# An attention and mixture-of-experts kernel: one rounding on another engine, one group of maxima and the weight loads at other places

## The chip, the core and the metric

The kernel runs on one core of a Trainium2 chip. The metric is the device time of one execution in microseconds; the runs shown are three executions of the kernel before, and one more that was profiled.

## What is computed

The input is 8 batches of 8 heads, 576 positions, 64 channels. Attention is causal with a decay, and its output, read as 4608 tokens of 512 channels, goes through a soft mixture of 8 experts with 4 slots each:

```
scores = (q @ k.T) / sqrt(64) + cum[i] - cum[j]      # cum = cumsum(log f); j > i is masked
attn   = softmax(scores); y = attn @ v               # per head
x      = y.transpose(0, 2, 1, 3).reshape(4608, 512)
logits = x @ phi                                     # 32 slots
slots  = softmax(logits over tokens).T @ x
out    = softmax(logits over slots) @ (relu(slots @ w1) @ w2)
```

## The kernel before

Heads are worked on in pairs: 32 pairs `g`, four to a batch, head `i` = 2g or 2g+1. All work is written out by hand in the order in which each engine takes it; the order of the code is the order of every engine's queue, and semaphores alone join the engines.

For a head there are two products. The first (`s1`, line 230) gives scores with queries on partitions, of which VectorE takes a maximum for each query (`tops`, lines 244 and 246, a group of instructions into `MT`, each with a short read-out of its own). `first(i, n)` is both for one of four groups of blocks. The maxima of a pair are turned into a row on TensorE (`mturn`, line 256), copied on ScalarE to `mr`, and carried by a DMA into a row of `YA` (`mrows`, lines 265 and 268). The second product (`s2`, lines 283 and 284) gives scores with keys on partitions; it uses that row to subtract the maximum. ScalarE makes exponentials of them (`expo`, line 290), GpSimd sets what lies above the diagonal to zero (`causal`, lines 298 and 301), and TensorE multiplies with the values (`s3`, line 315) 50 units for a pair, each in two passes. `both(i, n)` is `s2` and `expo` of a quarter.

The products are made of a rounded part and a rest. `round_k` and `round_q` (lines 183 and 188, ScalarE) round `RAW` into `WA` and `YA`; `dup_k` and `dup_q` (lines 199 and 203) copy these by DMA into `WB` and `YB`; `low_k` and `low_q` (lines 209 and 214, GpSimd) subtract to get the rests. `load_cum` (line 194) brings the cumulated logarithms.

The opening handles heads 0 and 1, the maxima of heads 2 to 4, and the values of pair 0. Behind it a loop over g = 1 to 31 does `s2` and `s3` of pair g beside the maxima of later heads. All loads and copies are issued by SyncE (SP) from one queue, in the order written. `wload(n)` (line 128) brings one of 27 weight tiles, 128 partitions of 4096 bytes, used only by the experts after the loop. In an iteration, SyncE's queue holds `RAW` of pair g+3 and `V` of pair g+1, a weight tile, the row of maxima, the logarithms of pair g+3, and the two copies of pair g+2.

Of the kernel before, what the change touches and what calls it, by code (L numbers as in the profile page):

```python
# [28 lines left out]
NRES = 27  # L29
# [19 lines left out]
def pt_col(c, i):  # L49
    at = {}  # L50
    for bank, cc, i0, w in SEGS:
        o = at.get(bank, 0)
        at[bank] = o + w
        if cc == c and i0 <= i < i0 + w:
            return SEG_O[bank] + o + i - i0
    raise ValueError


def queries(t, u):

    if t == 4:
        return 8
    return 2 * u + t if t < 2 else 4 + 2 * (1 - u) + t - 2


def units(h, u, ts):

    return [(h, t, u, c) for t in ts for c in range(queries(t, u) // 2 + 1)]


SIDES = [[x for n in zip(units(h, 0, range(4)), units(h, 1, range(4))) for x in n] for h in range(2)]
LAST = [units(h, h, (4,)) for h in range(2)]
# [3 lines left out]
def attn_softmoe(ctx: ExitStack, tc: tile.TileContext, qk, v, f, phi, w1, w2, cst, out):  # L76
    nc = tc.nc
# [21 lines left out]
    YA, WA, YB, WB = {}, {}, {}, {}  # L99
# [6 lines left out]
    RAW = [per.tile([P, 2, S], F32, name=f"RAW{i}") for i in range(3)]  # L106
# [19 lines left out]
    def wload(n):  # L126
        i, q = divmod(ORDER[n], 4)
        nc.sync.dma_start(quarter[n], (w1, w2)[i % 2][i // 2][:, QW * q : QW * q + QW])
# [25 lines left out]
    def pair(g):  # L154
        return 0 <= g < NG

    def head(i):
        return 0 <= i < NH
# [17 lines left out]
    def load_v(g):  # L176
        if pair(g):
            nc.sync.dma_start(V[:, g % 2], v[g])

    def round_k(g, *hs):  # L180
        if pair(g):
            for h in hs or range(2):
                nc.scalar.copy(WA[g % 3][0:64, S * h : S * h + S], RAW[g % 3][64:128, h])  # L183

    def round_q(g, *hs):
        if pair(g):
            for h in hs or range(2):
                nc.scalar.copy(YA[g % 3][0:64, h, 64:640], RAW[g % 3][0:64, h])  # L188
# [12 lines left out]
    def dup_q(g, h0=0, h1=2):  # L201
        if pair(g):
            nc.sync.dma_start(YB[g % 2][0:64, h0:h1].bitcast(F32), YA[g % 3][0:64, h0:h1, 64:640].bitcast(F32))
# [55 lines left out]
    def mrows(g, h0=0, h1=2):  # L259

        if not pair(g):
            return
        n = NBLK * (h1 - h0)
        mr = small.tile([2 * NBLK, P], F32R, name=f"mr{g}_{h0}", tag="mr", bufs=1)
        nc.scalar.copy(mr[0:n], st["pm", g, h0][0:n, 0:128])
        m = TOP[g % 3]
        dst = YA[g % 3][m : m + 1, h0:h1].rearrange("c h s -> c (h s)")
        nc.sync.dma_start(dst.bitcast(F32), mr[0:n].bitcast(F32))
# [18 lines left out]
    def expo(i, bank):  # L287
        if head(i):
            t, at = st["bank"]
            nc.scalar.activation(PT[i % 2][:, SEG_O[bank] : SEG_O[bank] + at], t[:, 0:at], AF.Exp, scale=0.125)  # L290
# [20 lines left out]
    def s3(g, todo):  # L311
        for h, t, u, c in todo:
            r = queries(t, u)
            at = pt_col(c, 64 * r)
            nc.tensor.matmul(  # L315
                pvv[h][64 * u : 64 * u + 64, t, :], PT[h][:, at : at + 64], V[:, g % 2, c, 65 * h : 65 * h + 65], start=(c == 0), stop=(c == r // 2)
            )
# [190 lines left out]
    def warm(n, a, w=192):  # L508

        for _ in range(n):  # L510
            nc.tensor.matmul(ring[0][:, 0:w], a[:, 0:128], a[:, 0:w], start=True, stop=True)
# [87 lines left out]
    def first(i, n, busy=0):  # L599
        s1(i, *GROUPS[n])  # L600
        warm(busy, cs)
        tops(i, *GROUPS[n])

    def both(i, n):
        s2(i, *((0,), (1,), (2,), (3, 4, 5))[n])
        expo(i, n)
# [15 lines left out]
    both(0, 1)  # L622
    first(2, 0)
    both(0, 2)
    nc.vector.tensor_copy(YA[1][0:64, 1, 64:640], RAW[1][0:64, 1])
    next(r1)
    first(2, 1)
    next(r1)
    s2(0, 3, 4, 5)
    round_k(1, 1)  # L630
    expo(0, 3)
    dup_q(1, 1, 2)
    dup_k(1, 1, 2)
# [18 lines left out]
    first(3, 2)  # L652
    first(3, 3)
    round_k(2, 0)
    both(1, 3)
    causal(1)
    low_k(3)
    low_q(3)
    round_q(2, 0)
    s3(0, SIDES[0])  # L660
    mturn(1, 1, 2)
    mrows(1, 1, 2)
    first(4, 0)
    round_k(2, 1)
    round_q(2, 1)
    dup_q(2)
    dup_k(2)
    s3(0, LAST[0])
    norm(0)
    first(4, 1)  # L670
    s3(0, LAST[1] + SIDES[1][:8])
# [53 lines left out]
    for g in range(1, NG):  # L725
        h0, h1 = 2 * g, 2 * g + 1
        u0, u1 = h0 + 3, h0 + 4
        b, w = divmod(g - 4, NPAIR)
        c = b - 1 if w == 0 else b if (b, w) == (B - 2, 3) else None
        if g < 4:  # L730
            load_v(g + 1)
            load_qk(g + 3)
        else:
            load_qk(g + 3)
            load_v(g + 1)
        if 2 <= g < NRES + 2:
            wload(g - 2)
        if w == 1:
            weigh(b)
        low_q(h0 + 2)  # L740
        low_q(h1 + 2)
        s2(h0, 0)
        expo(h0, 0)
        norm(h0 - 1)
        if w == 1:
            mgroup(b)
        if w == 2:
            combine(b, 0)
        s1(u0, 2)
        tops(u0, 2)  # L750
        s2(h0, 1)
        expo(h0, 1)
        s1(u0, 3)
        tops(u0, 3)
        if 1 < g < NG - 1:
            px(g - 1, 0)
        s2(h0, 2)
        expo(h0, 2)
        if g == NG - 1:
            px(g - 1, 0)  # L760
        if g > 1:
            px(g - 1, 3)
        else:
            round_k(3, 0)
            round_q(3, 0)
        s1(u0, 0, 1)
        tops(u0, 0, 1)
        if g > 1:
            px(g - 1, 1)
        s2(h0, 3)  # L770
        if g > 1:
            xcopy(g - 1, (0, 3))
            px(g - 1, 2)
            xcopy(g - 1, (1, 2))
        s2(h0, 4)
        s1(u0, 4, 5)
        s2(h0, 5)
        expo(h0, 3)
        tops(u0, 4, 5)
        causal(h0)  # L780
        low_k(h0 + 2)
        if w == 1:
            mtop(b)
        s2(h1, 0)
        expo(h1, 0)
        if g == 1:
            for t in (0, 3, 1, 2):
                px(0, t)
        px(g - 1, 4)
        if g == 1:  # L790
            xcopy(0, (0, 3))
            xcopy(0, (1, 2))
        xcopy(g - 1, (4,))
        s1(u1, 2)
        tops(u1, 2)
        s2(h1, 1)
        expo(h1, 1)
        s1(u1, 3)
        tops(u1, 3)
        s2(h1, 2)  # L800
        if g < NG - 2:
            expo(h1, 2)
        mturn(g + 1)
        mrows(g + 1)
        if g >= NG - 2:
            expo(h1, 2)
        s1(u1, 0, 1)
        tops(u1, 0, 1)
        s2(h1, 3, 4)
        s1(u1, 4, 5)  # L810
        s2(h1, 5)
        expo(h1, 3)
        tops(u1, 4, 5)
        causal(h1)
        low_k(h1 + 2)
        if g == 1:
            round_k(3, 1)
            round_q(3, 1)
        load_cum(g + 3)
        dup_q(g + 2)  # L820
        dup_k(g + 2)
        if g == 29:
            sides[2].close()
            p2 = fresh(ctx, "p2", 2)
            wstream(*p2, RAW[30 % 3])
        if g == 30:
            sides[1].close()
            xp = ctx.enter_context(tc.tile_pool(name="xp", bufs=1))
            X.append(xp.tile([P, NBLK, 256], F32, name="X3"))
            p0 = fresh(ctx, "p0", 1)  # L830
            p1 = fresh(late, "p1", 3)
            wstream(*p0, *p1, RAW[31 % 3])
        if g == 31:
            sides[0].close()
            with tc.using_default_side("right"):
                tp = ctx.enter_context(tc.tile_pool(name="tp", bufs=1))
            cT = tp.tile([P, sum(CUT)], F32R, name="cT")
            wstream(tp.tile([P, QW], F32, name="w36"))
        if w == 1:
            mcast(b)  # L840
        if c is not None:
            combine(c, 1)
        if w == 2 and b < B - 2:
            dispatch(b, *range(NBLK))
        if g == NG - 1:
            st["lg", B - 1] = scratch(False, f"lg{B - 1}")
            nc.vector.memset(st["lg", B - 1][:, 128:192], -1.0e30)
        round_k(g + 3)
        if w == 1:
            weigh2(b)  # L850
            total(b)
        round_q(g + 3)
        if c is not None:
            combine(c, 2)
        s3(g, VALUES[:30])
        norm(h0)
        if g == 31:
            logits(B - 1, 0, 1)
            wstream(XTS[:, 0:QW], PTS[:, 0:QW])
            split(0, 0)  # L860
            split(1, 0)
        s3(g, VALUES[30:])
        if w == 0:
            logits(b, *range(NPAIR))
        if w == 1:
            tokens(b, 0, 1)
        if g == 28:
            wstream(RAW[29 % 3])
# [272 lines left out]
```

## Time and profile before

| what | value |
|---|---|
| time, median of three runs | 389.6 us (389.45 to 389.81) |
| time of the profiled execution | 392.3 us |
| its span, first to last instruction | 390.6 us |
| TensorE busy | 370.5 us, 95% of the span |
| VectorE, ScalarE, GpSimd busy | 281.7, 271.3, 255.0 us |
| DMA | 93.72 MB, mean 240 GB/s |

In the profile, PE is TensorE's matmuls and PEld its weight loads, which overlap; DVE is VectorE, ACT ScalarE, POOL GpSimd, SP SyncE (SPq: its queue, which issues DMAs). A busy share is a mean over stages with different limits, so it is read by stretches of time. A releaser in brackets is the work that ended a wait, as far as the semaphores' events tell.

### The profile page before, as it was taken

What the parts mean: (1) busy time and instruction counts of PE and PEld (TensorE: products, weight loads), DVE (VectorE), ACT (ScalarE), POOL (GpSimd) and SP (SyncE); (2) the same over time, 40 slices, a digit from 0 to 9 for tenths busy, and PEclk for the clock granted to TensorE, in tenths of its full rate; (3) what the DMA queues carried; (4) which work ended last, traced back from release to release, by engine and by line L of the source; (5) the groups of instructions that cost most, each with busy time, mean ns of one, the idle gap of its engine ahead of it and who ended that gap; (6) DMA issues with size and microseconds to landing.
All of it is one profiled execution on the core that took longest, in us unless ns stands there. A gap on an engine that the chain in (4) does not pass through costs nothing.

```text
span 390.6 us, 15123 instructions
## 1 busy us (share of the span) xinstructions
PE 370.5 (95%) x5863; PEld 330.7 (85%) x5863; DVE 281.7 (72%) x1080; ACT 271.3 (69%) x669; POOL 255.0 (65%) x357
## 2 busy tenths in 40 slices
PE   7999999999999999999999999999999998999870
PEld 7789999999999999999999999999999885567640
DVE  7978887878887788788878887878787534341681
ACT  8869887878787778787878787878786553021560
POOL 4897887878787878787878787878787821000000
PEclk9999999999999999999999999999999998999995
DMA  6875978777777777777777777777775899995798
GB/s 205 205 195 148 283 223 278 189 233 207 224 211 215 213 212 214 213 214 211 213 214 214 211 214 212 214 214 212 212 227 154 269 350 377 407 417 206 264 393 314
DMA packets 34344, 93.72 MB, mean 240 GB/s; under 512 B 4266, under 2 KB 8288, under 8 KB 34272
## 3 DMA queue, kind: packets, MB, share of 16 engines
q1 hardware_dynamic: 34272, 92.75, 76.4%
q8 instruction: 46, 0.75, 0.8%
q14 instruction: 26, 0.21, 0.2%
HBM read 63.93 MB, written 9.73 MB: 189 GB/s over the span
## 4 chain that ended last, share of the span: by engine, by line
PE 86%; DMA 6%; POOL 2%; DVE 1%; ACT 1%; issue 1%; POOLq 0%; DVEq 0%; ACTq 0%
PE pv L315 24%; PE ring L283 14%; PE s L230 13%; PE ring L284 13%; PE pv L342 5%; PE pv L981 4%; PE more L941 4%; PE lg L389 3%; DMA out<-RAW 3%; PE ds L475 2%; DMA YA<-mr 2%; DMA WB<-WA 1%; POOL WB L209 1%; DMA PTS<-in_f 1%; POOL YB L214 1%
## 5 line engine op out<-in xcount | busy, mean ns | idle before, releaser
L290 ACT ACTIVATE PTS<-ring 128x320 f32<-128x320 f32 (+2 forms) x256 | 118.1, 502 | 49.3 <-PE ring L284 36.4
L283 PE MATMUL ring<-YA,WA 67*128 67x320 f32 (+9 forms) x384 | 121.5, 330 | 0.8 <-DMA YA<-mr 0.8
L246 DVE CUSTOM_DVE_ANT_0 s<-s,mask 128x320 f32<-128x320 f32 (+3 forms) x256 | 109.0, 442 | 5.6 <-PE s L230 1.1
L284 PE MATMUL ring<-YB,WB 128*128 128x320 f32 (+4 forms) x384 | 110.4, 296 | 0.0
L315 PE MATMUL pv<-V,PTS 128*64 128x65 f32 x3200 | 101.9, 223 | 0.2 <-POOL WB L209 0.2
L315 PEld LDWEIGHTS pv<-V,PTS 128*64 128x64 f32 x3200 | 96.9, 138 | 3.1 <-issue 1.5
L230 PE MATMUL s<-WA,YA 66*128 66x288 f32 (+9 forms) x384 | 98.2, 310 | 0.8 <-DMA RAW<-in_qk 0.4
L209 POOL TENSOR_TENSOR WB<-RAW,WB 64x576 fp32r<-64x576 f32 x64 | 90.4, 1412 | 11.1 <-DMA WB<-WA 5.8
L214 POOL TENSOR_TENSOR YB<-RAW,YA 64x576 fp32r<-64x576 f32 x64 | 89.7, 1421 | 2.6 <-POOL EX L397 0.2
L283 PEld LDWEIGHTS ring<-YA,WA 67*128 67x128 f32 (+3 forms) x384 | 69.7, 183 | 6.3 <-issue 2.1
L284 PEld LDWEIGHTS ring<-YB,WB 128*128 128x128 f32 (+1 forms) x384 | 70.0, 182 | 0.1
L230 PEld LDWEIGHTS s<-WA,YA 66*128 66x128 f32 (+1 forms) x384 | 62.9, 190 | 7.4 <-ACT PTS L290 1.5
L301 POOL TENSOR_SCALAR_AFFINE_SELECT PTS<-PTS 128x128 f32<-128x128 f32 (+1 forms) x128 | 31.5, 268 | 21.1 <-ACT PTS L290 18.6
L246 DVE DVE_READ_ACCUMULATOR2_ANT MT<- 128x1 fp32r x310 | 43.8, 141 | 0.0
L298 POOL TENSOR_SCALAR_AFFINE_SELECT PTS<-PTS 128x384 f32<-128x384 f32 x64 | 33.5, 523 | 14.2 <-ACT PTS L290 10.3
L342 PE MATMUL pv<-cs,X 128*128 128x128 f32 x155 | 42.0, 277 | 0.0
L183 ACT CAST WA<-RAW 64x576 fp32r<-64x576 f32 x64 | 40.1, 668 | 1.0 <-DMA RAW<-in_qk 0.2
L188 ACT CAST YA<-RAW 64x576 fp32r<-64x576 f32 x63 | 39.6, 671 | 0.4
L246 DVE CUSTOM_DVE_ANT_0 s<-s,mask,MT 128x288 f32<-128x288 f32 x62 | 32.6, 526 | 9.3 <-PE s L230 0.4
L330 DVE TENSOR_SCALAR rl<-pv 128x5 f32<-128x5 f32 x64 | 10.5, 164 | 34.0 <-PE pv L315 23.6
L335 DVE TENSOR_TENSOR X<-pv,rl 128x320 f32<-128x320 f32 (+1 forms) x65 | 31.5, 486 | 2.4 <-DMA YA<-mr 0.3
L244 DVE TENSOR_REDUCE MT<-s 128x1 fp32r<-128x288 f32 x62 | 27.8, 449 | 0.4 <-PE s L230 0.4
(221 smaller groups left out, 389.2 us busy)
## 6 DMA issues: line engine op xcount, KB each, us to landing
w<-in_w SPq DMA_DIRECT2D x45, 512.0 KB
RAW<-in_qk SPq DMA_DIRECT2D x31, 576.0 KB
V<-in_v SPq DMA_DIRECT2D x32, 325.0 KB
YB<-YA SPq DMA_DIRECT2D x30, 288.0 KB
WB<-WA SPq DMA_DIRECT2D x30, 288.0 KB
p<-in_w SPq DMA_DIRECT2D x6, 512.0 KB
out<-RAW SPq DMA_DIRECT2D x6, 512.0 KB
out<-p SPq DMA_DIRECT2D x5, 512.0 KB
```

What stands on the lines that cost most here:

```text
L183: nc.scalar.copy(WA[g % 3][0:64, S * h : S * h + S], RAW[g % 3][64:128, h])
L188: nc.scalar.copy(YA[g % 3][0:64, h, 64:640], RAW[g % 3][0:64, h])
L209: nc.gpsimd.tensor_tensor(t[0:64], RAW[g % 3][64:128, h], t[64:128].bitcast(F32), op=ALU.subtract)
L214: nc.gpsimd.tensor_tensor(YB[g % 2][64:128, h], RAW[g % 3][0:64, h], YA[g % 3][0:64, h, 64:640].bitcast(F32), op=ALU.subtract)
L230: nc.tensor.matmul(t[:, o : o + w], ya[0:m, h, 128 * blk : 128 * blk + 128], wa[0:m, j0 : j0 + w], start=True, stop=True)
L246: nc.vector.tensor_tensor_reduce(out=t[:, o : o + w], in0=t[:, o : o + w], in1=mask[:, m0 : m0 + w], scale=1.0, scalar=top.bitcast(F32) if ...
L283: nc.tensor.matmul(o, wa[0:m, j0 : j0 + n], ya[0:m, h, 64 + i0 : 64 + i0 + w], start=True, stop=False)
L284: nc.tensor.matmul(o, wb[:, j0 : j0 + n], yb[:, h, i0 : i0 + w], start=False, stop=True)
L290: nc.scalar.activation(PT[i % 2][:, SEG_O[bank] : SEG_O[bank] + at], t[:, 0:at], AF.Exp, scale=0.125)
L298: nc.gpsimd.affine_select(d3, d3, pattern=[[0, 3], [1, 128]], compare_op=ALU.is_ge, fill=0.0, base=0, channel_multiplier=-1)
L315: nc.tensor.matmul(pvv[h][64 * u : 64 * u + 64, t, :], PT[h][:, at : at + 64], V[:, g % 2, c, 65 * h : 65 * h + 65], start=(c == 0), stop= ...
L342: nc.tensor.transpose(pm[:, 0:128], x[:, t, 128 * (p % 2) : 128 * (p % 2) + 128], ident)
```

## The change

Three edits. In the opening, the rounding of the second head of pair 1 goes from VectorE (line 625) to ScalarE, behind the rounding of its keys. Also in the opening, the rounding of the queries of pair 2's first head stands ahead of `both(1, 3)` and no longer behind it, and pair 2's first maxima, `first(4, 0)`, stand ahead of the turn of head 3's maxima; `SIDES[0]` has 20 units, so the values of pair 0 are cut as before. In the loop, `wload` is issued behind `mrows`.

```diff
     both(0, 2)
-    nc.vector.tensor_copy(YA[1][0:64, 1, 64:640], RAW[1][0:64, 1])
     next(r1)
     first(2, 1)
     next(r1)
     s2(0, 3, 4, 5)
     round_k(1, 1)
+    round_q(1, 1)
     expo(0, 3)
     dup_q(1, 1, 2)
...
     round_k(2, 0)
+    round_q(2, 0)
     both(1, 3)
     causal(1)
     low_k(3)
     low_q(3)
-    round_q(2, 0)
-    s3(0, SIDES[0])
+    s3(0, SIDES[0][:20])
+    first(4, 0)
     mturn(1, 1, 2)
     mrows(1, 1, 2)
-    first(4, 0)
     round_k(2, 1)
     round_q(2, 1)
     dup_q(2)
     dup_k(2)
-    s3(0, LAST[0])
+    s3(0, SIDES[0][20:] + LAST[0])
...
             load_v(g + 1)
-        if 2 <= g < NRES + 2:
-            wload(g - 2)
         if w == 1:
...
         mturn(g + 1)
         mrows(g + 1)
+        if 2 <= g < NRES + 2:
+            wload(g - 2)
```

ScalarE's queue in the opening, with the changes marked; `WA_86` and `YA_85` are pair 1's rounded keys and queries, the 512 wide `ACTIVATE` is `expo(0, 3)`:

```order
 L594 CAST YA_89<-ring_151 2x128
 L183 CAST WA_86<-RAW_96 64x576
+L188 CAST YA_85<-RAW_96 64x576
 L290 ACTIVATE PTS<-ring_152 128x512
 L290 ACTIVATE PTS<-ring_153 128x448
```

One instruction came in ahead of `expo(0, 3)`; VectorE's queue lost line 625 ahead of head 2's maximum of block 4.

TensorE's queue at the values of pair 0, with the changes marked; `s_0` is head 4's first group of scores, `pv_150<-turner` the turn of head 3's maxima:

```order
 L284 MATMUL ring_153<-YB_91,WB_92 64x64
 L315 MATMUL pv_149<-V,PTS 64x65 x20
+L230 MATMUL s_0_395<-WA_94,YA_93 128x320
+L230 MATMUL s_0_395<-WA_94,YA_93 128x192
 L256 MATMUL pv_150<-turner,MT_110 5x128
-L230 MATMUL s_0_399<-WA_94,YA_93 128x320
-L230 MATMUL s_0_399<-WA_94,YA_93 128x192
 L315 MATMUL pv_149<-V,PTS 64x65 x5
```

Two matmuls went from behind the turn to ahead of it.

SyncE's queue in the loop, at the end of pair 2 and in pair 3, with the changes marked; `mr` is the row of maxima, `w` a weight tile:

```order
 L178 DMA V<-in_v 128x650
 L174 DMA RAW_97<-in_qk 128x1152
+L268 DMA YA_89<-mr_0_681 1x10x128
 L128 DMA w_113<-in_w 128x1024
-L268 DMA YA_89<-mr_0_682 1x10x128
```

The weight tile went from ahead of the row of maxima to behind it, and so directly ahead of the logarithms and the two copies; the same holds in the 26 pairs that follow.

## Rows read from the trace of the kernel before

**Rows 1.** Windows: stretch, length, then each engine's busy time, PEclk, DMA share, GB/s

```profile
16.00:18.00 2.00, 1.63 (x12) 1.30 (x11) 1.85 (x5) 1.41 (x4) 1.86 (x6) 1.00 0.94 336
18.00:20.00 2.00, 1.72 (x10) 1.23 (x10) 1.90 (x9) 1.38 (x5) 1.84 (x5) 1.00 1.01 204
...
32.00:310.00 278.00, 276.98 (x4706) 260.15 (x4707) 220.51 (x881) 220.84 (x548) 225.50 (x307) 1.00 0.74 216
```

**Rows 2.** Waits of PE, 30 to 310 us: sum, times, longest

```profile
PE ring L283 <- DMA YA<-mr: 0.5, 1, 0.5
```

**Rows 3.** Timeline of DVE in the opening: start, length, instruction

```profile
15.43 1.32 DVE L625 CAST YA<-RAW 64x576 fp32r<-64x576 f32 x1
16.67 0.44 DVE L244 TENSOR_REDUCE MT<-s 128x1 fp32r<-128x288 f32 x1
...
18.61 0.14 DVE L246 DVE_READ_ACCUMULATOR2_ANT MT<- 128x1 fp32r x1
...
19.52 0.14 DVE L246 DVE_READ_ACCUMULATOR2_ANT MT<- 128x1 fp32r x1
```

**Rows 4.** Groups by line and form, DVE: busy us, mean ns, idle before

```profile
L557 DVE CAST PTS<-PTS 64x576 fp32r<-64x576 f32 x1 | 0.5, 457 | 0.0
```

**Rows 5.** Timeline of PE and PEld in the opening; in brackets idle time and releaser

```profile
16.94 0.19 PEld L230 LDWEIGHTS s<-WA,YA 66*128 66x128 f32 x1 [0.67 <-POOL YA L578]
...
18.13 0.49 PE L511 MATMUL ring<-cs 128*128 128x192 f32 x2
...
18.89 0.22 PE L256 MATMUL pv<-turner,MT 128*5 128x128 f32 x1 [0.28 <-POOL WB L209]
...
19.71 0.30 PEld L230 LDWEIGHTS s<-WA,YA 66*128 66x128 f32 x2 [0.23 <-DVE MT L246]
...
22.20 0.50 PE L230 MATMUL s<-WA,YA 66*128 66x320 f32 x2
```

**Rows 6.** Timeline of ACT in the opening

```profile
16.09 0.67 ACT L183 CAST WA<-RAW 64x576 fp32r<-64x576 f32 x1
16.67 0.59 ACT L290 ACTIVATE PTS<-ring 128x512 f32<-128x512 f32 x1
17.82 0.94 ACT L290 ACTIVATE PTS<-ring 128x448 f32<-128x448 f32 x2 [0.57 <-ACT PTS L290]
...
21.48 0.67 ACT L188 CAST YA<-RAW 64x576 fp32r<-64x576 f32 x1
```

**Rows 7.** Timeline of SP's queue and of POOL in the opening

```profile
16.78 0.47 SPq L203 DMA_DIRECT2D YB<-YA  x1
...
17.93 0.45 SPq L194 DMA_DIRECT2D WA<-cumd  x1
...
21.88 0.49 POOL L301 TENSOR_SCALAR_AFFINE_SELECT PTS<-PTS 128x128 f32<-128x128 f32 x2
```

**Rows 8.** Chain that ended last: start, length, work (DMA: issue to landing)

```profile
5.82 4.61 DMA WB<-WA
...
97.03 3.07 PE pv L315 x100
...
126.45 3.80 DMA YA<-mr
```

**Rows 9.** Windows of two stretches in the loop, columns as in rows 1

```profile
127.00:129.00 2.00, 2.00 (x76) 2.00 (x74) 1.05 (x6) 1.96 (x4) 1.83 (x4) 1.00 0.07 15
95.00:96.00 1.00, 1.00 (x9) 0.94 (x9) 0.83 (x4) 0.96 (x5) 0.75 (x3) 1.00 0.99 379
```

**Rows 10.** The page's DMA issues: count and size of one

```profile
w<-in_w SPq DMA_DIRECT2D x45, 512.0 KB
```

**Rows 11.** Timeline of SP's queue and of POOL in a short pair

```profile
90.10 1.48 SPq L199 DMA_DIRECT2D WB<-WA  x1
...
95.74 1.42 POOL L209 TENSOR_TENSOR WB<-RAW,WB 64x576 fp32r<-64x576 f32 x1
...
97.82 0.49 POOL L301 TENSOR_SCALAR_AFFINE_SELECT PTS<-PTS 128x128 f32<-128x128 f32 x2
```

## Prediction

> **What bounds the kernel now.** I read the busy time of each engine by stretches first. From 32 to 310 us, the attention loop, TensorE is busy for 276.98 of 278.00 us [rows 1]: there is about 1 us in it that any edit to the loop can take away. In the opening it is not so full: 1.63 us of the two from 16 to 18, and 1.72 of the two from 18 to 20 [rows 1], 0.65 us idle. So the change can only pay in these few microseconds of the opening, or in single waits of the loop. The list of TensorE's waits over the loop names one of note, 0.5 us for the row of maxima that a DMA carries from `mr` into `YA` [rows 2]. What is gained early is kept: TensorE is the bound behind it, and whatever follows starts earlier by as much.
>
> **Which engine holds TensorE in the opening.** VectorE makes the row maxima there one behind the other. Between two of them it does the rounding of line 625, from 15.43 us, for 1.32 us, and only at 16.67 takes the next maximum (head 2, block 4) [rows 3]. The same kind of copy with the same shape, line 557, took 0.457 us earlier [rows 4]. TensorE's first wait there, the weight load at 16.94, is for a GpSimd memset [rows 5], which the change leaves where it is. Two others stand behind VectorE. The turn of head 2's maxima (line 256) begins at 18.89 after 0.28 us of idleness [rows 5]; the last of those maxima is read out at 18.61 to 18.75 [rows 3]. (The timeline blames a GpSimd operation; the program makes this instruction wait for VectorE and for a copy of `turner` on GpSimd that is long done, so I take VectorE.) Then the weight load for head 3's block 3 stands still for 0.23 us, until 19.71, for a buffer that VectorE reads until 19.66 [rows 3, 5].
>
> **The rounding's move.** ScalarE gets one more instruction, line 188, which takes it 0.67 us at 21.48, as line 183 does at 16.09 [rows 6]. It stands behind line 183, which runs 16.09 to 16.76, so it ends at about 17.45. What is queued behind: `expo(0, 3)`, at 16.67 before, then about 17.46 to 18.05; `expo(1, 0)` behind it, 17.82 before, then about 18.07 [rows 6]. Head 3's first matmul needs the rounded rows; it comes near 17.57, so it loses nothing or a tenth. VectorE loses 1.24 us of work (15.43 to 16.67). It then must wait for matmuls in between, the last piece of head 2's block 0 among them, which waits for a GpSimd memset and doesn't come earlier; I put the end of head 2's maxima at about 17.8 in place of 18.75, and that of head 3's first group at about 19.1 in place of 19.66. So the 0.28 goes whole, and the 0.23 nearly whole: 0.28 + 0.23 = 0.51 us. The bounds: nothing, if another releaser takes over; at most 0.66, if the turn follows the filler matmul of 18.13 after 0.26 us [rows 5], at 18.39 (0.50 earlier), and the weight load gains 0.16 more.
>
> The SyncE queue waits for the rounding too: the copy of `YA` into `YB` is issued at 16.78, when VectorE is through, and the cumulated logarithms of pair 2 behind it at 17.93 [rows 7]. With ScalarE they go out about 0.68 us later, if nothing else holds the queue.
>
> **`round_q(2, 0)` and `first(4, 0)`.** Before, the rounding of pair 2's queries follows `expo(1, 3)`, at 21.48 to 22.15 [rows 6], and pair 2's first maxima begin at 22.20 [rows 5]: that start is set by ScalarE. Put ahead of `expo(1, 3)`, the rounding follows `round_k(2, 0)` and is done near 21.1; `expo(1, 3)` goes 0.67 us later than it else would, ends near 21.7 and is needed by GpSimd only at 21.88 [rows 7]. `first(4, 0)` can then follow the 40 passes of values without a stop, so the 0.5 us isn't lost again; I count no further gain for it. It swaps places with the turn of head 3's maxima, which go out a little later and are used only in the next pair; nothing.
>
> A rule of the Trainium skill bears on the rounding. The row says 1.32 us, with a GpSimd subtraction under way. The Trainium skill (SBUF — State Buffer, SBUF: two separate sides) says that VectorE and GpSimd share a port pair as an exclusive lock, and that ScalarE never waits on anyone there. By it VectorE would get back more than the bare copy, and ScalarE's price stays 0.67; the trace agrees, 1.32 against 0.457 us for one shape. By the bare copy alone, VectorE would be only 0.46 us earlier and the gain about 0.4 us.
>
> **The weights behind the row of maxima.** It removes nothing; in 27 pairs, 2 to 28, one issue on SyncE (about 0.44 us) and one transfer of 512 KB change places with the row's. SyncE's queue waits for ScalarE's `mr` anyway, so the row is issued no earlier. Does the row land earlier? In the one case where TensorE waited, it took 3.80 us from issue to landing [rows 8], but the DMA engines were busy for only 7% of the time from 127 to 129 us [rows 9]: the weights, issued at the pair's start, were through. So I give the move no gain there: 0, at most the 0.5.
>
> Its cost is what now stands behind the weights: the cumulated logarithms, and the copies `YB<-YA` and `WB<-WA` of the next pair. At the 379 GB/s of a full stretch [rows 9], the 512 KB [rows 10] take 1.38 us, part of which falls in the hole that the DMAs leave beside the row. So the copies land between 0.44 (the issue alone) and 1.8 us later (issue and transfer in full); I take 0.9. In a short pair `WB<-WA` is issued at 90.10, and GpSimd's subtraction `low_k` begins at 95.74, 5.64 later [rows 11]; the longest such copy on the chain took 4.61 us [rows 8], which leaves 1.03. Behind `low_k` stands the causal fill of the odd head, 97.82 to 98.31 [rows 11]. The value matmuls from 97.03 take 3.07 us for 100 passes [rows 8] and reach the first that needs it after 54, at 98.69: 0.38 us of room more. So 1.4 us of lateness cost nothing: 0 for my 0.9, and 0.4 us in each short pair for 1.8. I take seven such pairs, one a batch: 2.8 us at the worst. The next `RAW` stands behind the copies as well; there ScalarE would wait, and I put that under the same bound.
>
> The Trainium skill (DMA: Bandwidth & Descriptors, Queues, rings and completion order) says that a DMA engine consumes the descriptors of one ring in order. That speaks against this part of the change: bytes which nobody needs for long go ahead of copies that are. It is what the third rival is made of.
>
> **The sum.** 0.51 of the opening, nothing for the rest: the profiled execution would go from 392.3 us (its span is 390.6) to 391.8. The median of the runs shown is 389.6, 2.7 below the profiled one; less 0.5 it gives **389.1 us**.
>
> **The rivals.**
> - The wait for the row of maxima goes too, because its DMA no longer shares the engines with the weights: 0.5 + 0.5, 388.6 us. For it: it is the loop's only long wait. Against: the DMA engines were idle then. 20%.
> - The opening's gain is taken back. The queue's 0.68 us make pair 2's logarithms land later than `first(4, 0)` can use them; issued at 18.6, and landing as slowly as that 3.80, they would come at 22.4, past the 22.20 of before. Then only GpSimd's chain and this DMA set the opening: 389.5 to 389.7. Against: the DMAs there are backlogged (the share is 1.01 from 18 to 20 [rows 1]), so a later issue need not mean a later landing. 18%.
> - Slower: the copies behind the weights come more than 1.4 us late in the short pairs, GpSimd's fill holds the value matmuls, seven times 0.4 less 0.5: 391.9; 0.2 each, 390.5. The sign turns at 0.07 us a pair, and 0.18 make it slower by over 0.2%. For it: the transfers are dense in the loop (share 0.74 [rows 1]). Against: the hole beside the row takes part of the transfer. 12%.
> - My forecast, 50%, with 388.8 to 389.4 as its own range.
>
> **The numbers.** 0.2% of 389.6 is 0.78 us, about what a measurement of this kernel tells from no change. Faster than 388.8: the first rival's 20% and the low edge of my forecast, 7%, together 27%. Slower than 390.4: the third rival, 12%. The rest, 61%, is the same. The range must leave out no more than a tenth on either side: 388.4 below (the first rival and its 0.66 bound), 390.2 above (the third at its mild end).
>
> **What would show it.** In the changed profile VectorE should take head 2's first maximum of block 4 near 15.6, and line 256 should start without a wait near 18.4. Pair 2's first maxima should start near 21.7 in place of 22.20. The loop's busy share should stand as it was, and GpSimd's `low_k` should begin as soon behind its fill as before. I am wrong if line 256 still waits (then GpSimd was the releaser), if `first(4, 0)` waits for a DMA, or if waits on GpSimd turn up ahead of the value matmuls in every fourth pair.

## The result, and the profile after

The changed kernel takes **394.5 us** (median of 4, 393.41 to 395.73) where the kernel before, on the same chip, takes 389.58 (median of 4): 1.0126 of it, interval 1.0096 to 1.0157. It is slower by 4.9 us, and the prediction of 389.1 is wrong, past its range; what happened is the mechanism of the slower rival, which it had priced at 0.9 to 2.3 us over the kernel before. The profiled execution after has a span of 392.6 us. Against the 390.6 of before that looks like 2.0 only: before's profiled execution was 2.7 above its median, and from pair 31's start to the end it took 78.3 us against 77.0 after, with a granted clock of 0.93 from 310 to 330 us (a mean: from 328 to 330 us it was 0.50, the lower of its two levels, 1.2 GHz; after: 1.00).

The opening first: VectorE's timeline in the changed kernel (start, length, instruction).

```profile
15.55 0.46 DVE L244 TENSOR_REDUCE MT<-s 128x1 fp32r<-128x288 f32 x1
```

And TensorE's there (in brackets idle time and what ended it):

```profile
17.48 0.51 PE L230 MATMUL s<-WA,YA 66*128 66x320 f32 x2 [0.37 <-ACT YA L188]
...
18.34 0.36 PE L256 MATMUL pv<-turner,MT 128*5 128x128 f32 x1
...
21.45 0.50 PE L230 MATMUL s<-WA,YA 66*128 66x320 f32 x2
```

VectorE takes the maximum of block 4 at 15.55, not 16.67 [rows 3]; line 256 starts without a wait at 18.34 (18.89 [rows 5]) and pair 2's maxima at 21.45 (22.20 [rows 5]). One wait is new: head 3's matmul at 17.48 waits 0.37 us for ScalarE's rounding. Another is gone, that of 16.94 [rows 5], which I had expected to stay. Most of this is no work of the change, as "The opening again" below shows. Windows of the changed kernel, columns as in [rows 1]:

```profile
16.00:18.00 2.00, 1.63 (x11) 1.21 (x10) 1.46 (x7) 1.97 (x5) 1.85 (x5) 1.00 0.95 347
18.00:20.00 2.00, 2.00 (x17) 1.88 (x16) 1.37 (x6) 1.74 (x5) 1.92 (x4) 1.00 0.89 207
32.00:310.00 278.00, 275.22 (x4648) 258.18 (x4645) 218.95 (x874) 217.56 (x539) 221.26 (x301) 1.00 0.75 212
```

The opening's hole from 18 to 20 is closed, and the loop has lost: TensorE is busy for 275.22 us where it was busy for 276.98 [rows 1]. TensorE's waits in the changed loop, 30 to 310 us (sum, times, longest):

```profile
PE pv L315 <- POOL PTS L301: 1.5, 5, 0.5
PE ring L283 <- DMA YA<-mr: 0.8, 1, 0.8
```

And GpSimd's, of which the first profile of the kernel before has none of this kind (a second, below, has 0.5 us in two):

```profile
POOL WB L209 <- DMA WB<-WA: 8.9, 12, 1.8
```

TensorE's value matmuls now wait for GpSimd's fill, and GpSimd's `low_k` for the copy `WB<-WA`. (Three more waits of `low_k`, 3.1 us, the profile puts down to ScalarE's `mr`; by the completion marks these too end 0.14 us behind the last share of the copy.) The wait for the row of maxima is still there, at 0.8 us. The chain that ended last shows how the two hang together, in pair 8 (start, length, work):

```profile
90.10 6.29 DMA WB<-WA
...
96.52 1.42 POOL WB L209
...
98.00 0.52 POOL PTS L298
98.52 0.45 POOL PTS L301 x2
...
99.02 1.50 PE pv L315 x42
```

The copy goes out at 90.10, as it did before [rows 11], but lands 6.29 us later; `low_k` starts at 96.52, not 95.74 [rows 11], the fill behind it ends at 98.97, and the last 42 value matmuls stand until then. The same piece stands in the chain at 42.81, 129.34, 216.69, 246.78 and 286.33. TensorE's timeline at this place, in the kernel before and in the changed one:

```profile
96.96 3.14 PE L315 MATMUL pv<-V,PTS 128*64 128x65 f32 x100
```
```profile
96.58 1.96 PE L315 MATMUL pv<-V,PTS 128*64 128x65 f32 x58
99.02 1.50 PE L315 MATMUL pv<-V,PTS 128*64 128x65 f32 x42 [0.47 <-POOL PTS L301]
```

Of the 0.79 us that the value matmuls take longer, only 0.47 are listed as a wait; the rest is in the two halves, which take 3.46 us together. So the 1.5 us of waits above stand for a greater loss. Where the time goes is read from the starts of the pairs (the first matmul of line 283, 448 wide, in TensorE's timeline; differences to the kernel before worked out):

```
start of pair         2      4      9      13     22     25     29     31
before              35.57  53.07 101.47 140.45 226.61 255.79 294.29 312.28
changed kernel      -0.71  -0.28  +0.41  +1.28  +2.30  +2.73  +3.21  +3.32
opening only        -0.60  -0.59  -0.66  -0.99  -1.02  -0.99  -0.99  -1.14
low_k twice         -0.79  -0.67  +1.50  +2.10  +4.52  +5.78  +6.90  +6.43
```

From pair 2 to pair 31 the changed kernel loses 4.0 us. 3.7 of it come in six steps, each over one pair: 0.42 (pair 3), 0.81 (8), 0.55 (12), 0.71 (21), 0.74 (24), 0.49 (28). These six are those of the chain's pieces. A seventh, 0.3 in pair 11, is the longer wait for the row. Against the opening-only profile, which differs by the move of the weights alone, the loss over the same pairs is 4.6. (The last two lines are experiments, below.)

### The profile page after: what moved, and what is told of

Its sections match the earlier page's. It is cut to its first block, busy times and chain, and to the rows that moved or that the text cites. A ratio compares the mean times of both kernels' runs of the same rounds, so it can differ in the third digit from the quotient of the medians.

```text
span 392.6 us, 15124 instructions
## 1 busy us (share of the span) xinstructions
PE 370.8 (94%) x5863; PEld 331.1 (84%) x5863; DVE 281.0 (72%) x1079; ACT 271.9 (69%) x670; POOL 253.6 (65%) x357
## 4 chain that ended last, share of the span: by engine, by line
PE 75%; DMA 13%; POOL 4%; ACT 2%; DVE 2%; issue 1%; SPq 0%; POOLq 0%; ACTq 0%; DVEq 0%
PE pv L315 20%; PE ring L283 11%; PE s L230 11%; PE ring L284 10%; DMA WB<-WA 10%; PE pv L981 4%; PE more L941 4%; PE pv L342 3%; DMA out<-RAW 3%; POOL WB L209 3%; PE lg L389 2%; PE ring L511 2%; PE ds L475 2%; DMA YA<-mr 1%; POOL PTS L301 1%
## 5 line engine op out<-in xcount | busy, mean ns | idle before, releaser
L315 PE MATMUL pv<-V,PTS 128*64 128x65 f32 x3200 | 104.1, 223 | 1.8 <-POOL PTS L301 1.5
L315 PEld LDWEIGHTS pv<-V,PTS 128*64 128x64 f32 x3200 | 98.3, 138 | 5.6 <-POOL PTS L301 2.4
```

Of the source, the lines that this page charges most:

```text
L315: nc.tensor.matmul(pvv[h][64 * u : 64 * u + 64, t, :], PT[h][:, at : at + 64], V[:, g % 2, c, 65 * h : 65 * h + 65], start=(c == 0), stop= ...
```

## The experiments

The chips of these runs gave the kernel before 390.5 to 390.9 us, so only ratios are compared.

**Opening only.** The weight load back at the pair's start:

```diff
             load_v(g + 1)
+        if 2 <= g < NRES + 2:
+            wload(g - 2)
...
         mrows(g + 1)
-        if 2 <= g < NRES + 2:
-            wload(g - 2)
```

> The changed kernel with the weight load back at the pair's start; the opening's edits alone. Theory A (the weights' bytes go ahead of the copies YB<-YA and WB<-WA, GpSimd's low_k then waits for the copies, and the odd head's causal fill and the value matmuls behind it): the whole loss goes, and the opening's gain stays: 0.7 us under the kernel before, 388.7 to 389.1 beside 389.6; no wait of low_k in the loop. Theory B (the loop, begun 0.7 us earlier, falls into another phase with its DMAs, and the loss comes from that): most of the loss stays, 393 to 395.

0.9995 [0.998, 1.001], 390.17 us. The whole loss is gone, and theory B with it. But of the 0.7 us that the opening had gained in the one pair of profiles the times show 0.2 at their middle, and can't tell that from nothing.

**Weights only.** The kernel before with the other part alone (`wload` behind `mrows`, the opening untouched).

> The kernel before with the weight load behind the row of maxima; the opening as it was. Theory A: 394.8 to 396, that is the changed kernel's time plus about 0.7, and low_k waits about 1 us in the short pairs. Theory B: about 389.6, as before.

1.0122 [1.0094, 1.0151]: the move of the weights alone is the loss, all of it. Its waits of TensorE and GpSimd, 30 to 310 us:

```profile
PE pv L315 <- POOL PTS L301: 3.0, 2, 2.0
POOL WB L209 <- DMA WB<-WA: 9.5, 10, 2.8
```

Its time is not the changed kernel's plus 0.7, as expected, but the same. Which pairs pay differs from profile to profile: here pair 3 loses 1.27 us and pair 8 2.36, and pair 12 nothing. Nor did its opening need the edits: line 625 started at nearly the same moment there, but GpSimd's work beside it was 0.8 us earlier, and pair 2 began 0.61 us earlier than in the first profile of the same code. VectorE's timeline in this run:

```profile
15.40 0.55 DVE L625 CAST YA<-RAW 64x576 fp32r<-64x576 f32 x1
```

**The opening again.** Two runs for this: the kernel before once more, and the kernel before with only `round_q(1, 1)` on ScalarE:

```diff
-    nc.vector.tensor_copy(YA[1][0:64, 1, 64:640], RAW[1][0:64, 1])
...
     round_k(1, 1)
+    round_q(1, 1)
```

> The kernel before, unchanged, for a second look at its opening. If the 1.32 us of line 625 belongs to the program, it is there again, with pair 2's start at 35.5 us. If it was a collision with GpSimd in that execution, line 625 takes 0.5 to 0.6 us, TensorE doesn't wait ahead of line 256, and pair 2 starts near 34.9.

> The kernel before with only the one rounding moved from VectorE to ScalarE; pair 2's maxima, the values and the weights as before. My prediction's opening term says 0.5 us less: 0.9987 of the kernel before. The rival, from the weights-only run, whose line 625 took 0.55 us and whose pair 2 began 0.6 us early without any of the opening's edits: 1.32 us was a collision of one execution, and the move is worth 0.1 us or nothing: 0.9995 to 1.0005.

In the kernel before, profiled again:

```profile
15.40 0.58 DVE L625 CAST YA<-RAW 64x576 fp32r<-64x576 f32 x1
```

0.58 us, and pair 2 starts at 34.89 (35.57 in the first profile). With the rounding moved pair 2 starts at 34.96 and the time is 0.9991 [0.9965, 1.0018]: no gain that these runs can tell. So 1.32 us was one execution's: GpSimd's subtraction there ran from 15.01 to 16.43, and the cast ended 0.32 us behind it; in the weights-only run it ran from 14.22 to 15.64, and the cast ended 0.31 behind it, after only 0.24 us of overlap at its start. GpSimd was late in the first profile because its first subtraction waited for a copy, the one of 4.61 us [rows 8]:

```profile
10.57 1.40 POOL L209 TENSOR_TENSOR WB<-RAW,WB 64x576 fp32r<-64x576 f32 x1 [5.80 <-DMA WB<-WA]
```

In the eleven other profiles it starts at 9.16 to 10.43. Where the rounding stays on VectorE without this collision, line 256 starts earlier than with the move: at 18.12 in the kernel before again, at 18.06 in the run with `low_k` twice (below), and in weights only at

```profile
18.09 0.22 PE L256 MATMUL pv<-turner,MT 128*5 128x128 f32 x1
```

beside 18.34, 18.33 and 18.33 in the changed kernel, opening only and rounding only. By pair 2 the two can't be told apart: it starts at 34.78 to 34.96 in the first three and at 34.86 to 34.97 in the others.

**How late the copies come.** Three versions of the changed kernel: the weights behind `WB<-WA` as well; one eighth of them (64 KB) behind the row, the rest at the pair's start; and half and half.

```diff
-            wload(g - 2)
...
         dup_k(g + 2)
+        if 2 <= g < NRES + 2:
+            wload(g - 2)
```
```diff
             load_v(g + 1)
+        if 2 <= g < NRES + 2:
+            wload(g - 2, 128, QW)
...
-            wload(g - 2)
+            wload(g - 2, 0, 128)
```

(the second with 512 in place of 128 for the halves)

> The changed kernel with the weight load behind WB<-WA, so that the cumulated logarithms and both copies go ahead of it and only the next RAW stands behind it. Theory A: low_k no longer waits; what is left is the RAW's lateness for ScalarE: 388.8 to 390.5. Theory A2 (the late RAW, by which ScalarE's rounding waits, is what costs, and not the late copies): 393 to 395, as the changed kernel.

> The changed kernel with the weight load cut in two: seven eighths of the columns at the pair's start, one eighth (64 KB) behind the row of maxima. Theory A (the bytes): 389 to 390. Theory C (the issue's place in SyncE's queue, some 0.4 us by which everything behind it goes out later): still 393 to 395.

> The changed kernel with the weight load cut in two halves of 256 KB, one at the pair's start and one behind the row of maxima. If there is a room and a threshold: the copies come about 1 us late and cost little, 0.999 to 1.003 of the kernel before. If the loss goes with the bytes: half of the 1.26%, 1.005 to 1.008.

And one that leaves the bytes and the place in the code and takes another queue, ScalarE's:

```diff
-            wload(g - 2)
+            wload(g - 2, nc.scalar)
```

> The changed kernel with the loop's weight loads issued by ScalarE on its own queue, at the same place behind mr. The bytes and the moment stay, only the copies no longer stand behind them in SyncE's queue. If the order within one queue makes the copies late: the loss goes, 0.998 to 1.001 of the kernel before, and WB<-WA takes 3.9 to 4.6 us as before. If the DMA engines' time shared between all queues does it: the copies stay late and 1.005 to 1.013 is left.

All in one table. The middle columns are worked out from the completion marks of the 27 copies `WB<-WA` issued between 40 and 300 us (from the issue of the row ahead of one until the last of its 16 shares is done) and from `low_k`'s idle times over 0.15 us:

```
weights behind the row        row's issue to copy done   low_k waits   of the kernel before
                              median (range), us         count, sum
none (before)                 6.51 (6.19 to 7.88)         0,  0.0
none, behind WB<-WA           6.56 (6.23 to 7.98)         1,  0.2      1.0010 [0.9998, 1.0022]
512 KB, ScalarE's queue       6.57 (6.28 to 7.87)         0,  0.0      1.0060 [1.0033, 1.0086]
64 KB                         6.88 (6.59 to 8.15)         1,  0.6      0.9998 [0.9983, 1.0013]
256 KB                        7.04 (6.67 to 8.67)         1,  0.6      1.0001 [0.9987, 1.0015]
512 KB (changed kernel)       8.47 (7.64 to 10.10)       15, 12.1      1.0126 [1.0096, 1.0157]
512 KB (weights only)         8.38 (7.57 to 10.30)       11, 10.6      1.0122 [1.0094, 1.0151]
```

I take the 0.37 of 64 KB for the issue alone. 256 KB add 0.16 to it, 512 KB add 1.59: the first half of the load fits in beside the row, the second pushes the copies. There is a room, and a threshold between 256 and 512 KB, as the halves show; theory C falls with the eighth. With the weights last ScalarE waits for a late `RAW` longer than in any other, and the time is 0.10% longer (0.22 at the interval's upper end), which can't be told from nothing:

```profile
ACT WA L183 <- DMA RAW<-in_qk: 6.9, 9, 2.1
```

so theory A2 falls too.

On ScalarE's queue the copies come as before. But that doesn't show that the order in SyncE's queue makes them late, because the moment did not stay, as the expectation had it: ScalarE's queue issues the load while ScalarE's own work written ahead of it is still to come, 0.70 us ahead of the row at the median, and not 0.85 behind it. In pair 8 (`mr` is copied at 87.91):

```profile
87.47 0.34 ACTq L128 DMA_DIRECT2D w<-in_w  x1
```
```profile
88.18 0.81 SPq L268 DMA_DIRECT2D YA<-mr  x1
```

Worked out from the DMA packets (medians, from the issue of the row), the load runs from 0.28 to 2.86 us there, and the first packet of `YB<-YA` follows at 2.71, as in the kernel before (2.68); in the changed kernel the load runs from 1.93 to 4.79 and that packet comes at 3.65. So the load was all but through when the copies came. What the runs show is that 512 KB directly ahead of the copies make them late; whether by the order in one queue or by the bytes as such, none of them tells. That run loses in another place: issued just ahead of the row, the weights now make the row slow (2.90 us from issue to its last packet at the median, 1.54 before), and TensorE waits for it five times:

```profile
PE ring L283 <- DMA YA<-mr: 2.8, 5, 0.7
```

I had expected no loss there; it was the wrong half of the expectation.

**GpSimd alone.** No transfer is touched, but `low_k` is done twice in seven pairs of the kernel before:

```diff
         low_k(h0 + 2)
+        if w == 0:
+            low_k(h0 + 2)
```

> The kernel before, in which GpSimd does low_k of the next pair's even head twice, one behind the other, in every fourth pair (pairs 4, 8 to 28, seven in all); the second writes the same values again. No transfer is touched: GpSimd alone is 1.49 us later ahead of the odd head's fill. If the way of the loss is low_k, fill, value matmuls: the fill ends near 99.7 in place of 98.3, and the first value matmul that needs it, after some 52 passes from 96.96, near 98.6, waits about 1.1 us; seven times that is 7.8 us, 1.020 of the kernel before. If the fill has more room than that, or the wait is made up for later in the pair: under 2 us, 1.000 to 1.005.

1.0203 [1.0172, 1.0234], as worked out. TensorE's waits, 30 to 310 us:

```profile
PE pv L315 <- POOL PTS L301: 5.7, 7, 0.9
```

TensorE's timeline in pair 8, where the fill ends only near 100.0:

```profile
97.34 1.96 PE L315 MATMUL pv<-V,PTS 128*64 128x65 f32 x58
100.10 1.09 PE L315 MATMUL pv<-V,PTS 128*64 128x65 f32 x30 [0.80 <-POOL PTS L301]
```

The steps over the seven pairs are 1.05 to 1.24 us each, 7.95 in all. So the second half of the way, `low_k`, fill, value matmuls, is shown without any DMA.

**The fill first.** The changed kernel with the two turned round on GpSimd:

```diff
         causal(h0)
-        low_k(h0 + 2)
...
         causal(h1)
+        low_k(h0 + 2)
         low_k(h1 + 2)
```

> The changed kernel with GpSimd's low_k of the next pair's even head written behind the odd head's causal fill, so that a low_k which waits for WB<-WA no longer holds the fill. Theory A1 (the copies' lateness reaches TensorE by GpSimd's order: copy, low_k, fill, value matmuls): of the about 4.8 us that the changed kernel loses most comes back, what stays is the late RAW's 0.6: 1.001 to 1.004 of the kernel before. Theory A2 (it reaches TensorE by another way, by the late RAW and ScalarE or by the logits' and weights' own work): 1.008 to 1.013, as the changed kernel.

1.015 [1.0085, 1.0215]: no better than the changed kernel, from which it can't be told. The time alone would speak for A2 and against A1; the waits of TensorE say otherwise:

```profile
PE tk L457 <- POOL EX L432: 7.0, 7, 1.2
```

The copies are as late as before (8.55 us at the median), but there is no wait for the fill any more, and pairs 3, 8, 12, 24 and 28, which had lost 0.42 to 0.81 us each, now lose 0.03 at most. But GpSimd's copy `EX` of line 432 comes later by this order, and TensorE waits for it 1 us once a batch. As a cure it failed; that the steps vanish from the pairs where they stood bears theory A1 out.

No version here beats the kernel before: opening only, rounding only, the weights last, the eighth and the halves can't be told from it.

## Why the prediction was wrong, point by point

- **The failed step** is the cost of what stands behind the weights: "1.4 us of lateness cost nothing: 0 for my 0.9". The mechanism was named there, and as the third rival; both sizes in it were off. The lateness is 1.96 us at the median (6.51 to 8.47), over my pick of 0.9 and just over my upper bound of 1.8. And the room was too wide: I measured it on one copy, 4.61 us [rows 8], taken for the longest, and a copy of the opening at that. By their completion marks the copies of the kernel before take 4.12 to 5.59 us in the loop, and between a copy's end and `low_k` there are 0.41 us (the copy of 244.39) to 1.75 in the pairs that I called short (every fourth, 4 to 28), where I had 1.03. The 0.38 us of room behind `low_k` were right: in pair 8 TensorE came 0.4 us earlier and `low_k` 0.8 later, 1.2 together, of which 0.8 were lost. What lies beyond that room costs TensorE 0.4 to 0.8 us a pair, 3.7 in six, where my worst case said 2.8 in seven; two of the six (3 and 21) are not short ones. The median of the times lost 4.9, 0.9 more than this one pair of profiles shows in the loop. Against the opening-only profile the loop loses 4.6, so 0.6 of the 0.9 lie in the first profile of before; the executions after lie 2.3 us apart, those of before 0.4, and the rest stays open.
- **The hole beside the row** ("part of which falls in the hole"): right in kind. It takes 256 KB at nearly no cost, and not the rest.
- **`RAW`** "under the same bound": it came late too (ScalarE's rounding waited 4.3 us in all in the changed loop); by the run with the weights last it costs 0.10%, which can't be told from nothing.
- **The move gains nothing:** right. The wait for the row is 0.8 us in the changed kernel, and the first rival falls. That wait does not go by the move: with the weights at the pair's start it is 0.5 to 0.6 in three profiles (before, before again, rounding only) and missing in two (opening only, `low_k` twice), and with the weights alone moved it is missing too.
- **The opening, 0.51 us:** wrong, though the trace did what the step said: line 256 came 0.55 earlier, at the 18.34 that I had put near 18.4, and pair 2 0.71. That was luck. I had taken the duration of line 625 and the wait of 0.28 from one execution, where GpSimd was late and the cast collided with it. In three others with the rounding on VectorE it took 0.52 to 0.58 us, and line 256 came at 18.06 to 18.12 without the edit. The wait at 16.94, for a memset that I said would come no earlier, was that execution's too. The move puts a wait of 0.37 us for ScalarE into head 3's matmul, where I allowed a tenth, and is worth too little to be told (0.2 us at the middle of the opening-only run).
- **The second rival** (the opening's gain is taken back): its outcome, but not its way. `first(4, 0)` starts at 21.45 without a wait for pair 2's logarithms.
- **The port rule** of the Trainium skill (SBUF — State Buffer, SBUF: two separate sides), an exclusive lock by which the loser waits for the whole instruction: the traces agree, the cast ended 0.32 and 0.31 us behind GpSimd's. I used it only for the gain; by it 1.32 us is also a duration that hangs on when the two meet, and that I passed over.
- **The rule on a ring's order** of the Trainium skill (DMA: Bandwidth & Descriptors, Queues, rings and completion order) carried the third rival, at 12%. The traces fit it: with the weights ahead of the copies in the one queue 8.47 us, with them behind 6.56. They don't single it out, since on the other queue (6.57) the load had all but run before the copies came.
- **`first(4, 0)` and `round_q(2, 0)`:** no gain, as counted; pair 2's maxima start at 21.45 and 21.59 with them (changed kernel, opening only) and at 21.44 and 21.59 without them (before again, rounding only).

## What to carry to other kernels

Moving a bulk load in a queue is priced at what will then stand behind it: follow each such transfer to the engine that waits for it, and to what stands behind that wait on its own engine. The room is the smallest over all its occurrences, not that of the one copy that the chain shows, and a lateness past it is paid again in every occurrence that has no room left. A duration or a wait of a few tenths that one execution shows on VectorE or TensorE is looked for in a second one before it becomes a term of a sum. And a run that moves a transfer to another queue is read for when the transfer ran: here that changed with the queue.

## What was not expected of the hardware

- The 16 shares of one copy end apart: in the changed kernel the first is done 0.5 us later than before, the last 1.96, and the last holds the wait. For `WB<-WA` the median of first to last is 0.42 us in the kernel before and 1.95 with 512 KB ahead of it (up to 3.52). Why one share falls back so far I have not settled.
- A load of 512 KB issued on another queue 0.70 us ahead of a row of 5 KB takes the row from 1.54 to 2.90 us; issued 0.85 us behind it in the same queue, it leaves it at 1.54.
